# Attention decode with gradients: scores as 512-column matmuls in four column groups, with q among 32 weight columns and rows spread by one-hot fp32 matmuls

One core of one Trainium2 chip. The metric is the device time of one execution in microseconds (us); the kernel before takes a median of 1289.56 us in 3 runs (1288.37 to 1290.94). "Per head" means per one of the 64 pairs of batch and head; a head has eight slots on TensorE, four for its k tile and four for its v tile, and a slot handles a chunk of 16 blocks of 128 rows.

## The reference

One query row per head attends to 8192 keys; wanted are the output and the gradients of q, k and v for a given output gradient.

```python
B, H, Sq, Sk, D = 2, 32, 1, 8192, 128          # all bfloat16
def forward(q, k, v):
    p = softmax(einsum("bhqd,bhkd->bhqk", q, k) * D ** -0.5)
    return einsum("bhqk,bhkd->bhqd", p, v)
out, vjp = jax.vjp(forward, q, k, v)
return out, *vjp(grad_out)                      # out, dq, dk, dv
```

k and v are read (268 MB) and dk and dv written (268 MB). Everything else is small.

## The kernel before

Each head's k and v come as tiles `[128, 64, 128]` of 2 MB; twelve such buffers rotate, and dk or dv is computed in place of k or v and stored from there. TensorE transposes 16 blocks at a time into PSUM, ScalarE copies them to SBUF (`ev`), and the scores are 16 matmuls, each with a transposed block as weights and one column of q as the moving data. The result already has the layout that softmax needs: score of row (p, n) at partition p, column n.

```python
def transpose_chunk(i, c):                       # one slot of TensorE
    ...
    for t in range(CH):                          # CH = 16
        nc.tensor.transpose(tp[:, t, :], src[:, c * CH + t, :], ident_bf[:])
    nc.scalar.copy(out=ev[:], in_=tp[:])

def score_chunk(i, c, ev):
    dst = h.dp if w else h.s                     # w = 0: q.k, w = 1: grad_out.v
    for t in range(CH):
        nc.tensor.matmul(dst[:, c * CH + t : c * CH + t + 1],
                         lhsT=ev[:, t, :], rhs=qdT[:, w, i : i + 1], start=True, stop=True)

def acc(i, w, c):                                # weighted sum of rows, two column groups
    for m in range(CH // QT):                    # QT = 4, so four 512-column matmuls
        nc.tensor.matmul(h.acc[w][g : g + CW, :], lhsT=wts[:, n0 : n0 + CW],
                         rhs=rows[:, n0 : n0 + QT, :] ...)

def outer(i, w, c, ends):                        # VectorE: dk or dv in place, then its store
    ...
    if w == 0 and i in SPREAD:                   # SPREAD = range(4, 60, 7): eight heads
        by_rows(store_eng, dst, h.tile[w], (P - 2, 2))   # store split into 126 + 2 rows
    else:
        eng.dma_start(out=dst[...], in_=h.tile[w][...])

# order of one slot in the main loop:
#   outer products; broadcast of q or grad_out; transposes of this chunk;
#   joins; acc (v, then k); max_spread + expo; scores of the chunk before; small sums
```

Of the kernel before, what the change touches and what calls it, by code (L numbers as in the profile page):

```python
# [11 lines left out]
BF16 = mybir.dt.bfloat16  # L12
F32 = mybir.dt.float32

CH = 16
QT = 4
CW = 64
NG = 2
NTILE = 12
FIRST = 6  # L20
SPREAD = range(4, 60, 7)
# [3 lines left out]
def kernel(  # L25
# [11 lines left out]
    nc = tc.nc  # L37
    B, H, Sq, D = q.shape
    Sk = k.shape[2]
    P = nc.NUM_PARTITIONS  # L40
    assert Sq == 1 and D == P
    BH = B * H
    assert BH <= P
    NT = Sk // P
    assert NT * P == Sk and NT % CH == 0
    NCH = NT // CH
    SL = 2 * NCH
# [4 lines left out]
    pin = tc.keep_in_program_order  # L52

    const = ctx.enter_context(tc.tile_pool(name="const", bufs=1))
    kvp = ctx.enter_context(tc.tile_pool(name="kv", bufs=1))
    evp = ctx.enter_context(tc.tile_pool(name="ev", bufs=2))
    work = ctx.enter_context(tc.tile_pool(name="work", bufs=1))
    small = ctx.enter_context(tc.tile_pool(name="small", bufs=2))
    ps_tp = ctx.enter_context(tc.tile_pool(name="ps_tp", bufs=2, space=bass.MemoryType.PSUM))
    ps_sdp = ctx.enter_context(tc.tile_pool(name="ps_sdp", bufs=1, space=bass.MemoryType.PSUM))  # L60
# [15 lines left out]
    heads = [Head() for _ in range(BH)]  # L76

    def slot_of(i, w):

        n = 2 * i + w  # L80
        return n if n < NTILE else slot_of(i - NTILE // 2, 1 - w)

# [7 lines left out]
    def load(i, w, pieces=(NCH,)):  # L90
        h = heads[i]
        t = kvp.tile([P, NT, D], BF16, tag=f"kv{slot_of(i, w)}", name="kvt")
        h.tile[w] = t
        src = (v_v if w else k_v)[i]
        c = 0
        for m in pieces:
            n0, n1 = c * CH, (c + m) * CH
            pin(load_eng.dma_start(out=t[:, n0:n1, :], in_=src[:, n0:n1, :]))  # L98
            c += m
# [4 lines left out]
    for w, a in enumerate((q, grad_out)):  # L104
        rows = a.rearrange("b h s d -> (b h s) d")
        r0 = FIRST if w == 0 else 0
        if r0:
# [3 lines left out]
                    out=qd_nat[:r0, w, :], in_=rows[:r0], max_dma_last_dim=D  # L111
# [4 lines left out]
    load(0, 1)  # L116
    for j in range(1, min(NTILE // 2, BH)):
        load(j, 0)
# [4 lines left out]
    ident_f = const.tile([P, P], F32)  # L123
    masks.make_identity(nc, ident_f[:])
    ones = const.tile([P, 1], F32)
    nc.vector.memset(ones[:], 1.0)
    groups = [g * P // NG for g in range(NG)]
    diag = const.tile([P, QT], F32)
# [7 lines left out]
    nc.vector.memset(E_pad[:], 0.0)  # L136
    nc.vector.memset(dS_pad[:], 0.0)

    qdT = const.tile([P, 2, BH], BF16)
    for w in range(2):  # L140
        tps = ps_m.tile([P, BH], BF16, tag=f"acc{w}", name="tps")
        nc.tensor.transpose(tps[:], qd_nat[:BH, w, :], ident_bf[:BH, :BH])
        nc.vector.tensor_copy(out=qdT[:, w, :], in_=tps[:])

    dqT = const.tile([P, BH], BF16)
    oT = const.tile([P, BH], BF16)

    def begin_s(i):

        h = heads[i]  # L150
        sw = ps_sdp.tile([P, NT + P + 1], F32, tag="s", name="sw")
        h.s = sw[:, 0:NT]
        h.mT = sw[0:1, NT : NT + P]
        h.mb = sw[:, NT + P :]

    def begin_dp(i):

        h = heads[i]
        dpw = ps_sdp.tile([P, NT + 2 + D], F32, tag="dp", name="dpw")
        h.dp = dpw[:, 0:NT]  # L160
        h.lsum = dpw[:, NT : NT + 2]
        h.qbp = dpw[:, NT + 2 :]

    def broadcast(i, w):

        h = heads[i]
        pin(
            nc.tensor.matmul(  # L168
                h.qbp,
                lhsT=qdT[:, w, i : i + 1].to_broadcast([P, P]),  # L170
                rhs=ident_bf[:],
                start=True,
                stop=True,
            )
        )
        h.qb[w] = small.tile([P, D], BF16, tag=f"qb{w}", name="qb")
        pin(nc.vector.tensor_copy(out=h.qb[w][:], in_=h.qbp))  # L177

    def transpose_chunk(i, c):
        w, c = divmod(c, NCH)  # L180
        src = heads[i].tile[w]
        tp = ps_tp.tile([P, CH, P], BF16, tag="tp", name="tp")
        for t in range(CH):
            pin(nc.tensor.transpose(tp[:, t, :], src[:, c * CH + t, :], ident_bf[:]))  # L184
        ev = evp.tile([P, CH, P], BF16, tag="ev", name="ev")
        pin(nc.scalar.copy(out=ev[:], in_=tp[:]))  # L186
        return ev

    def score_chunk(i, c, ev):
        h = heads[i]  # L190
        w, c = divmod(c, NCH)
        dst = h.dp if w else h.s
        for t in range(CH):
            pin(
                nc.tensor.matmul(  # L195
                    dst[:, c * CH + t : c * CH + t + 1],
                    lhsT=ev[:, t, :],
                    rhs=qdT[:, w, i : i + 1],
                    start=True,
                    stop=True,  # L200
                )
            )

    def max_part(i):
        h = heads[i]
        h.mp = small.tile([P, 1], F32, tag="mp", name="mp")
        pin(nc.vector.reduce_max(out=h.mp[:], in_=h.s, axis=AX.X))  # L207
# [120 lines left out]
    def acc(i, w, c):  # L328
# [6 lines left out]
        for m in range(CH // QT):  # L335
            n0 = c * CH + m * QT
            g = groups[m % NG]
            pin(
# [3 lines left out]
                    rhs=rows[:, n0 : n0 + QT, :].rearrange("p n d -> p (n d)"),  # L342
                    start=(c == 0 and m < NG),
                    stop=(c == NCH - 1 and m >= CH // QT - NG),
                )
# [42 lines left out]
    def outer(i, w, c, ends):  # L388

        h = heads[i]  # L390
        n0 = c * CH
        shape = [P, CH, D // 2, 2]
        pin(
            nc.vector.tensor_tensor(  # L394
                out=h.tile[w][:, n0 : n0 + CH, :].rearrange("p n (e t) -> p n e t", t=2),
                in0=h.qb[w][:]
                .rearrange("p (e t) -> p e t", t=2)
                .unsqueeze(1)
                .to_broadcast(shape),
                in1=h.pair[w][:, n0 : n0 + CH, :].unsqueeze(2).to_broadcast(shape),  # L400
                op=ALU.mult,
            )
        )
        if c + 1 in ends:
            at = ends.index(c + 1)
            b0, b1 = (ends[at - 1] if at else 0) * CH, (c + 1) * CH
            dst = (dv_v if w else dk_v)[i]
            if w == 0 and i in SPREAD:
                by_rows(store_eng, dst, h.tile[w], (P - 2, 2))
            else:  # L410
                eng = load_eng if len(ends) > 1 else store_eng
                pin(eng.dma_start(out=dst[:, b0:b1, :], in_=h.tile[w][:, b0:b1, :]))  # L412
# [6 lines left out]
    last = list(range(1, NCH + 1))  # L419
    AHEAD = NTILE // 2  # L420

    prev = None
    for g in range(SL * BH + O0 + NCH + 4 - SL):
        now = [(g // SL - b, g % SL + b * SL) for b in range(4)]
        now = [(i, r) for i, r in now if 0 <= i < BH]

        def at(r0):

            return next((i for i, r in now if r == r0), None)

        def within(r0):

            return next(((i, r - r0) for i, r in now if r0 <= r < r0 + NCH), None)

        if (i := at(O1 + NCH)) is not None and i + AHEAD < BH:
            load(i + AHEAD, 0)
        if (i := at(O0 + NCH)) is not None and i + AHEAD < BH:
            load(i + AHEAD, 1)
        if x := within(O1):
            outer(x[0], 1, x[1], last if x[0] == BH - 1 else whole)  # L440
        if x := within(O0):
            outer(x[0], 0, x[1], last if x[0] == BH - 1 else whole)
        ev = None
        if g < SL * BH:
            i, r = divmod(g, SL)
            if r == 0:
                begin_s(i)
            if r == 3:
                begin_dp(i)
                broadcast(i, 1)  # L450
            if r == 6:
                broadcast(i, 0)
            ev = transpose_chunk(i, r)
        if (i := at(A1 + NCH + 2)) is not None:
            join(i, 1)
        if (i := at(A0 + NCH + 2)) is not None:
            join(i, 0)
        if x := within(A1):
            acc(x[0], 1, x[1])
        if x := within(A0):  # L460
            acc(x[0], 0, x[1])
        if (i := at(NCH + 2)) is not None:
            max_spread(i)
            expo(i)
        if prev is not None:
            score_chunk(*prev)
        prev = (g // SL, g % SL, ev) if ev is not None else None

        if (i := at(NCH)) is not None:
            max_part(i)  # L470
        if (i := at(NCH + 1)) is not None:
            max_all(i)
        if (i := at(NCH + 3)) is not None:
            normalise_p(i)
        if (i := at(SL)) is not None:
            weigh(i)
        if (i := at(SL + 1)) is not None:
            normalise_ds(i)
        if (i := at(A1 + NCH)) is not None:
            pick(i, 1)  # L480
        if (i := at(A0 + NCH)) is not None:
            pick(i, 0)

    for w, (src, dst) in enumerate(((dqT, out_1), (oT, out_0))):
        tps = ps_m.tile([BH, P], BF16, tag=f"acc{w}", name="tps")
# [34 lines left out]
```

## Time and profile before

| | before |
|---|---|
| median of 3 runs | 1289.56 us |
| profiled run, a fast one | 1284.86 us (span 1283.1) |
| compulsory bytes | 536.9 MB |
| need of TensorE per head, first heads | 17.31 us |
| heads apart later, at the pace of the loads | 19.94 us |

The slices, waits and stretches stand in the prediction below. Four more lines of the page of the kernel before matter later: the busy times, two of the transfer queues (packets, MB, share of the 16 transfer engines' span), and the whole-tile stores (size, median us from issue to landing).

### The profile page before, as it was taken

How to read it: one execution, taken by the hardware profiler on the slowest of the kernel's cores; microseconds unless marked ns; L12 is line 12 of the kernel's file. 1: busy time of each engine (PE TensorE's matmuls, PEld its weight loads, DVE VectorE, ACT ScalarE, POOL GpSimd, SP SyncE). 2: the span in 40 equal slices, each digit the busy share in tenths (PEclk: the TensorE clock that was granted, in tenths of full speed). 3: DMA queues.
4: the chain of work that ended last, by engine and by line, in shares of the span. 5: the costliest groups of instructions: out<-in, count | busy, mean ns of one | idle time of the engine just before them, and what ended most of it. 6: DMA issues, size and time to landing. Idle time of an engine off the chain costs nothing.

```text
span 1283.1 us, 42576 instructions
## 1 busy us (share of the span) xinstructions
PE 1128.5 (88%) x19268; PEld 859.1 (67%) x19268; DVE 935.2 (73%) x2122; ACT 975.2 (76%) x641; POOL 76.0 (6%) x143
## 2 busy tenths in 40 slices
PE   6999999999988998898889898898889888989881
PEld 5777777667666766676666676676667666667650
DVE  2888888778777777686777687786767677777773
ACT  6888888778877877787777787786778677778750
POOL 0000000000000000000000000000000000000000
PEclk9999999999999999998999999998989899899985
DMA  9999999999999999999999999999999999999996
GB/s 388 422 428 426 428 426 427 428 428 425 428 428 425 418 427 428 428 421 427 428 426 425 426 429 428 425 425 429 427 425 421 423 427 428 423 425 426 428 409 267
DMA packets 40194, 539.68 MB, mean 421 GB/s; under 512 B 5196, under 2 KB 5196, under 8 KB 6476
## 3 DMA queue, kind: packets, MB, share of 16 engines
q1 hardware_dynamic: 20172, 272.70, 50.0%
q0 software_dynamic: 19840, 264.25, 48.8%
q8 instruction: 150, 2.46, 0.7%
q14 instruction: 32, 0.26, 0.0%
HBM read 268.47 MB, written 268.47 MB: 418 GB/s over the span
## 4 chain that ended last, share of the span: by engine, by line
DMA 33%; another core or an unknown queue 29%; PE 16%; issue 10%; DVE 8%; ACT 1%; SPq 1%; POOL 1%; POOLq 0%; DVEq 0%; ACTq 0%
DMA kvt<-in_v_dram 20%; DMA out_dram<-kvt 7%; PE tp L184 7%; DVE kvt L394 5%; DMA kvt<-in_k_dram 5%; PE acc L339 4%; PE dpw L195 2%; PE sw L195 2%; DVE sel L362 1%; ACT ev L186 1%; SPq L98 1%; DMA qd_nat<-in_q_dram 1%; PE dpw L282 1%; POOL out_dram L412 0%
## 5 line engine op out<-in xcount | busy, mean ns | idle before, releaser
L186 ACT COPY ev<-tp 128x2048 bf16<-128x2048 bf16 x512 | 954.4, 1865 | 268.8 <-PE tp L184 256.8
L184 PE MATMUL tp<-ident_bf,kvt 128*128 128x128 bf16 x8192 | 558.5, 223 | 96.6 <-DMA kvt<-in_v_dram 74.4
L394 DVE TENSOR_TENSOR kvt<-qb,pair 128x2048 bf16<-128x2048 bf16 x512 | 621.2, 1214 | 0.3
L184 PEld LDWEIGHTS <-kvt 128*128 128x128 bf16 x8192 | 489.8, 101 | 103.6 <-DMA kvt<-in_v_dram 77.8
L195 PEld LDWEIGHTS <-ev 128*128 128x128 bf16 x8192 | 243.2, 96 | 208.7 <-issue 149.1
L339 PE MATMUL acc<-kvt,dS_pad 128*64 128x512 bf16 x1024 | 166.8, 408 | 0.8 <-DVE dqT L379 0.8
L339 PE MATMUL acc<-kvt,E_pad 128*64 128x512 bf16 x1024 | 160.5, 394 | 0.0
L195 PE MATMUL dpw<-qdT,ev 128*128 128x1 bf16 x4096 | 140.7, 164 | 18.8 <-DVE qb L177 18.0
L362 DVE SCALAR_TENSOR_TENSOR sel<-acc,diag,sel 128x128 f32<-128x128 f32 x384 | 134.7, 351 | 13.6
L195 PE MATMUL sw<-qdT,ev 128*128 128x1 bf16 x4096 | 141.8, 164 | 1.2 <-ACT ev L186 1.2
L207 DVE TENSOR_REDUCE mp<-sw 128x1 f32<-128x64 f32 x64 | 14.4, 224 | 156.1 <-PE sw L195 156.1
L412 POOL DMA_DIRECT2D out_dram<-kvt x118 | 63.3, 536 | 1086.1 <-DVE kvt L394 818.4
L339 PEld LDWEIGHTS <-dS_pad 128*64 128x64 bf16 x1024 | 37.4, 110 | 24.4 <-issue 5.3
L247 DVE CAST E_pad<-E_f 128x64 bf16<-128x64 f32 x64 | 12.5, 195 | 54.5 <-ACT E_f L238 54.5
L339 PEld LDWEIGHTS <-E_pad 128*64 128x64 bf16 x1024 | 36.4, 108 | 21.3 <-issue 0.7
L376 PE MATMUL acc<-ones,sel 128*128 128x1 f32 x256 | 43.5, 239 | 6.2 <-DVE sel L362 6.2
L253 DVE CUSTOM_DVE_ANT_0 junk<-E_f,dpw 128x64 bf16<-128x64 f32 x64 | 14.1, 221 | 45.3 <-PE dpw L195 45.3
L282 PE MATMUL dpw<-ld,ones 128*128 128x1 f32 x256 | 46.3, 250 | 0.1
L376 PEld LDWEIGHTS acc<-ones,sel 128*128 128x128 f32 x256 | 39.3, 194 | 7.3 <-DVE sel L362 7.3
L356 DVE TENSOR_SCALAR sel<-acc,diag 128x128 f32<-128x128 f32 x128 | 44.1, 344 | 0.0
L177 DVE CAST qb<-dpw 128x128 bf16<-128x128 f32 x128 | 35.4, 277 | 6.2 <-PE dpw L168 6.2
L282 PEld LDWEIGHTS dpw<-ld,ones 128*128 128x128 f32 x256 | 38.2, 188 | 0.5 <-DVE ld L253 0.5
(44 smaller groups left out, 314.2 us busy)
## 6 DMA issues: line engine op xcount, KB each, us to landing
out_dram<-kvt POOLq DMA_DIRECT2D x118, 2048.0 KB, 68.0
kvt<-in_v_dram SPq DMA_DIRECT2D x64, 2048.0 KB, 19.4
kvt<-in_k_dram SPq DMA_DIRECT2D x63, 2048.0 KB, 19.7
out_dram<-kvt POOLq DMA_DIRECT2D x8, 2016.0 KB, 73.2
out_dram<-kvt SPq DMA_DIRECT2D x8, 512.0 KB, 22.1
kvt<-in_k_dram SPq DMA_DIRECT2D x2, 512.0 KB, 4.5
kvt<-in_k_dram SPq DMA_DIRECT2D x1, 1024.0 KB, 7.3
out_dram<-kvt POOLq DMA_DIRECT2D x8, 32.0 KB, 72.6
```

The source lines that it names most:

```text
L177: pin(nc.vector.tensor_copy(out=h.qb[w][:], in_=h.qbp))
L184: pin(nc.tensor.transpose(tp[:, t, :], src[:, c * CH + t, :], ident_bf[:]))
L186: pin(nc.scalar.copy(out=ev[:], in_=tp[:]))
L195: nc.tensor.matmul(dst[:, c * CH + t : c * CH + t + 1], lhsT=ev[:, t, :], rhs=qdT[:, w, i : i + 1], start=True, stop=True,)
L207: pin(nc.vector.reduce_max(out=h.mp[:], in_=h.s, axis=AX.X))
L282: nc.tensor.matmul(out, lhsT=ones[:].to_broadcast([P, P]), rhs=col, start=True, stop=True)
L339: nc.tensor.matmul(h.acc[w][g : g + CW, :], lhsT=wts[:, n0 : n0 + CW], rhs=rows[:, n0 : n0 + QT, :].rearrange("p n d -> p (n d)"), start=( ...
L356: nc.vector.tensor_scalar(out=h.sel[:], in0=block, scalar1=diag[:, 0:1], scalar2=None, op0=ALU.mult)
L362: nc.vector.scalar_tensor_tensor(out=h.sel[:], in0=block, scalar=diag[:, b : b + 1], in1=h.sel[:], op0=ALU.mult, op1=ALU.add,)
L376: nc.tensor.matmul(h.acc[w][:, 0:1], lhsT=h.sel[:], rhs=ones[:], start=True, stop=True)
L394: nc.vector.tensor_tensor(out=h.tile[w][:, n0 : n0 + CH, :].rearrange("p n (e t) -> p n e t", t=2), in0=h.qb[w][:] .rearrange("p (e t) -> ...
L412: pin(eng.dma_start(out=dst[:, b0:b1, :], in_=h.tile[w][:, b0:b1, :]))
```

## The change

The intent is to replace sixteen weight loads and one-column matmuls per slot by four 512-column matmuls. q becomes one of 32 weight columns; q's columns of the heads stand four apart with zeros between, so the window of 32 columns also holds the next heads' q. It starts c columns early for chunk c, so that the wanted scores of chunk c accumulate in row c of their group; the rows from 4 on belong to other heads and are never used. Four column groups of 32 write four row ranges of one PSUM bank and may run together. After four chunks the bank holds a head's scores as rows; VectorE copies it to SBUF, and four fp32 matmuls with one-hot columns pick rows 0 to 3 of each group and transpose them into the layout of before.

```diff
-    qdT = const.tile([P, 2, BH], BF16)
+    qdT = const.tile([P, 2, Q0 + NCH * BH + SW], BF16)      # q's columns NCH apart, zeros between
...
     def score_chunk(i, c, ev):
-        dst = h.dp if w else h.s
-        for t in range(CH):
+        q0 = Q0 + NCH * i - c
+        for g in range(SG):                                  # SG = 4, SW = 32
             pin(nc.tensor.matmul(
-                    dst[:, c * CH + t : c * CH + t + 1],
-                    lhsT=ev[:, t, :],
-                    rhs=qdT[:, w, i : i + 1],
-                    start=True, stop=True,
+                    h.raw[g * SW : (g + 1) * SW, :],
+                    lhsT=qdT[:, w, q0 : q0 + SW],
+                    rhs=ev[:, g * QT : (g + 1) * QT, :].rearrange("p n d -> p (n d)"),
+                    start=(c == 0), stop=(c == NCH - 1),
             ))
+    def keep_raw(i):
+        h.rows = work.tile([P, QT * P], F32, tag="rows", name="rows")
+        pin(nc.vector.tensor_copy(out=h.rows[:], in_=h.raw[:]))
+
+    def spread_rows(i, w):
+        for t in range(QT):
+            pin(nc.tensor.matmul(
+                    h.score[w].rearrange("p (n t) -> p n t", t=QT)[:, :, t],
+                    lhsT=h.rows[:, t * P : (t + 1) * P],
+                    rhs=sel4[:].rearrange("p c g -> p (c g)"), start=True, stop=True))
```

Both score areas, the transposed maximum, the sums and the broadcast of q and grad_out (`broadcast`) now share one PSUM bank, since `raw` needs one for itself. The maximum, the exponentials and everything after them come one slot later (cut here; in the main loop, `NCH + 2` becomes `NCH + 3` and so on). TensorE has 19268 matmuls before and 14148 after. (The trace lists each fp32 matmul twice.)

More of the change, by code (lines that the diff above doesn't have):

```diff
@@ L18 @@
 NG = 2
+SG = 4
+SW = 32
 NTILE = 12
@@ L137 @@
     nc.vector.memset(dS_pad[:], 0.0)
-    qdT = const.tile([P, 2, BH], BF16)
+    sel4 = const.tile([P, NCH, SG], F32)
+    nc.vector.memset(sel4[:], 0.0)
+    for g in range(SG):
+        nc.vector.tensor_copy(
+            out=sel4[g * SW : (g + 1) * SW, :, g],
+            in_=ident_f[g * SW : (g + 1) * SW, g * SW : g * SW + NCH],
+        )
+    Q0 = NCH - 1
+    qdT = const.tile([P, 2, Q0 + NCH * BH + SW], BF16)
+    nc.vector.memset(qdT[:], 0.0)
     for w in range(2):
@@ L142, with begin @@
         nc.tensor.transpose(tps[:], qd_nat[:BH, w, :], ident_bf[:BH, :BH])
-        nc.vector.tensor_copy(out=qdT[:, w, :], in_=tps[:])
+        nc.vector.tensor_copy(
+            out=qdT[:, w, Q0 : Q0 + NCH * BH].rearrange("p (i f) -> p i f", f=NCH)[:, :, 0],
+            in_=tps[:],
+        )
     dqT = const.tile([P, BH], BF16)
     oT = const.tile([P, BH], BF16)
-    def begin_s(i):
+    def begin(i):
         h = heads[i]
-        sw = ps_sdp.tile([P, NT + P + 1], F32, tag="s", name="sw")
-        h.s = sw[:, 0:NT]
-        h.mT = sw[0:1, NT : NT + P]
-        h.mb = sw[:, NT + P :]
-    def begin_dp(i):
-        h = heads[i]
-        dpw = ps_sdp.tile([P, NT + 2 + D], F32, tag="dp", name="dpw")
-        h.dp = dpw[:, 0:NT]
-        h.lsum = dpw[:, NT : NT + 2]
-        h.qbp = dpw[:, NT + 2 :]
+        sw = ps_sdp.tile([P, 2 * NT + 2 * P + 4], F32, tag="s", name="sw")
+        h.score = (sw[:, 0:NT], sw[:, NT : 2 * NT])
+        h.s, h.dp = h.score
+        h.mT = sw[0:1, 2 * NT : 2 * NT + P]
+        h.qbp = sw[:, 2 * NT + P : 2 * NT + 2 * P]
+        h.lsum = sw[:, 2 * NT + 2 * P : 2 * NT + 2 * P + 2]
+        h.mb = sw[:, 2 * NT + 2 * P + 2 : 2 * NT + 2 * P + 3]
     def broadcast(i, w):
@@ L169, in broadcast @@
                 h.qbp,
-                lhsT=qdT[:, w, i : i + 1].to_broadcast([P, P]),
+                lhsT=qdT[:, w, Q0 + NCH * i : Q0 + NCH * i + 1].to_broadcast([P, P]),
                 rhs=ident_bf[:],
@@ L191, in score_chunk @@
         w, c = divmod(c, NCH)
-        dst = h.dp if w else h.s
-        for t in range(CH):
+        if c == 0:
+            h.raw = ps_sdp.tile([P, QT * P], F32, tag="raw", name="raw")
+        q0 = Q0 + NCH * i - c
+        for g in range(SG):
             pin(
                 nc.tensor.matmul(
-                    dst[:, c * CH + t : c * CH + t + 1],
-                    lhsT=ev[:, t, :],
-                    rhs=qdT[:, w, i : i + 1],
+                    h.raw[g * SW : (g + 1) * SW, :],
+                    lhsT=qdT[:, w, q0 : q0 + SW],
+                    rhs=ev[:, g * QT : (g + 1) * QT, :].rearrange("p n d -> p (n d)"),
+                    start=(c == 0),
+                    stop=(c == NCH - 1),
+                )
+            )
+    def keep_raw(i):
+        h = heads[i]
+        h.rows = work.tile([P, QT * P], F32, tag="rows", name="rows")
+        pin(nc.vector.tensor_copy(out=h.rows[:], in_=h.raw[:]))
+    def spread_rows(i, w):
+        h = heads[i]
+        for t in range(QT):
+            pin(
+                nc.tensor.matmul(
+                    h.score[w].rearrange("p (n t) -> p n t", t=QT)[:, :, t],
+                    lhsT=h.rows[:, t * P : (t + 1) * P],
+                    rhs=sel4[:].rearrange("p c g -> p (c g)"),
                     start=True,
@@ L445 @@
             i, r = divmod(g, SL)
-            if r == 0:
-                begin_s(i)
-            if r == 3:
-                begin_dp(i)
+            if r == NCH:
+                begin(i)
                 broadcast(i, 1)
-            if r == 6:
+            if r == NCH + 2:
                 broadcast(i, 0)
@@ L461 @@
             acc(x[0], 0, x[1])
-        if (i := at(NCH + 2)) is not None:
+        if (i := at(NCH + 1)) is not None:
+            spread_rows(i, 0)
+        if (i := at(SL + 1)) is not None:
+            spread_rows(i, 1)
+        if (i := at(NCH + 3)) is not None:
             max_spread(i)
@@ L469 @@
         if (i := at(NCH)) is not None:
+            keep_raw(i)
+        if (i := at(SL)) is not None:
+            keep_raw(i)
+        if (i := at(NCH + 1)) is not None:
             max_part(i)
-        if (i := at(NCH + 1)) is not None:
+        if (i := at(NCH + 2)) is not None:
             max_all(i)
-        if (i := at(NCH + 3)) is not None:
+        if (i := at(NCH + 4)) is not None:
             normalise_p(i)
-        if (i := at(SL)) is not None:
+        if (i := at(SL + 1)) is not None:
             weigh(i)
-        if (i := at(SL + 1)) is not None:
+        if (i := at(SL + 2)) is not None:
             normalise_ds(i)
```

## The prediction

> **What bounds the kernel now.** I read the page's shares first: TensorE 88%, ScalarE 76%, VectorE 73% of 1283.1 us. That reads like a TensorE kernel. The slices below it say otherwise.
>
> ```profile
> PE   6999999999988998898889898898889888989881
> DMA  9999999999999999999999999999999999999996
> GB/s 388 422 428 426 428 426 427 428 428 425 428 428 425 418 427 428 428 421 427 428 426 425 426 429 428 425 425 429 427 425 421 423 427 428 423 425 426 428 409 267
> HBM read 268.47 MB, written 268.47 MB: 418 GB/s over the span
> ```
>
> The transfers stand at about 427 GB/s from the second slice to the last but two, whether TensorE shows a 9 or an 8. The bytes are the inputs and outputs themselves, 536.9 MB; at 427 GB/s they take 1257 us, and 26 us are left for the start and the end. So I looked at what TensorE does in its gaps: the table of waits.
>
> ```profile
> POOL out_dram L412 <- DVE kvt L394: 818.4, 89, 31.5
> ACT ev L186 <- PE tp L184: 256.8, 370, 9.3
> PE tp L184 <- DMA kvt<-in_v_dram: 74.4, 40, 5.5
> PE tp L184 <- DMA kvt<-in_k_dram: 22.2, 31, 1.5
> SPq L98 <- DMA out_dram<-kvt: 1139.0, 116, 25.1
> ```
>
> TensorE waits for loads (96.6 us), ScalarE for TensorE, and the load queue for stores that must land before a buffer is free (1139 us; the twelve 2 MB buffers are all in use). Stores take a median of 68.0 us from issue to landing, loads 19.4: seven or so tiles stand in the transfer queues. That is the slack: computation can be later by tens of us before a transfer is late.
>
> The table of stretches shows two regimes. First number: length, then busy time of PE, PEld, DVE, ACT, POOL, and at the end granted clock, DMA share, GB/s.
>
> ```profile
> 100.00:120.00 20.00, 19.68 (x360) 15.04 (x357) 17.25 (x39) 17.60 (x12) 1.88 (x3) 1.00 1.01 429
> 640.00:660.00 20.00, 17.11 (x303) 13.14 (x301) 14.37 (x34) 15.04 (x11) 1.93 (x3) 1.00 1.01 427
> 1260.00:1283.00 23.00, 0.90 (x3) 0.63 (x3) 0.92 (x5) 0.00 (x0) 0.00 (x0) 0.50 0.51 211
> ```
>
> Early, twelve tiles were loaded ahead and TensorE works them off at its own pace: starts of transposes from head to head lie 17.31 us apart for heads 1 to 12. From about 215 us on it gets ahead of the loads, and heads come 19.94 us apart (mean of heads 20 to 63). So the compute side has 17.31 us of need in a period of 19.94 us: **2.6 us per head of slack**. The end is fixed by the last tile, landed at 1233.5, its work until 1260, and stores that drain at half rate until 1283.
>
> **What the Trainium skill says.** "DMA: Bandwidth & Descriptors", section Bandwidth, gives a ceiling of 435 GB/s and 425 measured for one core; the trace's 427 agrees, so nothing is to be had there without fewer bytes. "TensorE: Matmul & The Clock Gate", Part 3, says that matmuls whose outputs lie in different column groups run at the same time (2.38 times for three groups at 512 columns). The trace agrees for two groups: below, four 512-column matmuls on two halves take 0.62 us, and the score work after them starts 0.55 us after their start; its Part 2 gives 216 ns for one, 0.86 us for four in a row. "TensorEngine Tiling (Array Packing)", Key Properties, says that changing the tiling mode drains the array: the trace has 0.31 us from the second pair's start to the first score matmul, where pair to pair is 0.24. Four groups are not in this trace; I rest on the page. "VectorE: DVE Perf Modes", the errata section, gives 120 + columns cycles at 0.96 GHz for a copy out of PSUM: 258 ns for 128 fp32 columns; the trace has 277.
>
> **The change, part by part.** One slot of TensorE (one chunk of 16 tiles; eight slots to a head) in the compute-bound stretch:
>
> ```profile
> 117.96 1.05 PE L184 MATMUL tp<-ident_bf,kvt 128*128 128x128 bf16 x16
> 118.94 0.62 PE L339 MATMUL acc<-kvt,E_pad 128*64 128x512 bf16 x4
> 119.50 0.55 PE L195 MATMUL sw<-qdT,ev 128*128 128x1 bf16 x16
> 119.92 1.05 PE L184 MATMUL tp<-ident_bf,kvt 128*128 128x128 bf16 x16
> ...
> 125.69 0.38 PE L218 MATMUL sw<-gm,ones 1*128 1x1 f32 x2
> 126.39 0.54 PE L195 MATMUL dpw<-qdT,ev 128*128 128x1 bf16 x16 [0.32 <-DVE qb L177]
> ```
>
> From start to start: transposes 0.98, accumulation 0.56, scores 0.41 us; 1.95 us, times 8 is 15.6, and the small fp32 matmuls and one wait make the 17.3.
>
> 1. Scores. Removed: 16 weight loads with one-column matmuls, 0.41 us. Added: four weight loads of 32 columns and four 512-column matmuls in four column groups, one wave. If the groups run together, the wave costs what the second pair does, 0.31 us to the next kind of work, perhaps 0.35. Estimate -0.08 x 8 = **-0.6 us per head**. The instruction order shows 2048 of them where 8192 were.
> 2. Spreading the rows. Eight fp32 matmuls per head (128x128 weights, 16 columns). The kernel has the like in its fp32 sums over partitions: at 111.43 two passes take until 111.65, 0.22 us per matmul, bound by the fp32 weight load, so that 16 columns for one should be nearly free. 8 x 0.22, plus two switches of mode at 0.1: **+2.0 us per head**.
> 3. Waits. The wait for the broadcast copy (about 0.4 us at 126.39) goes, as scores have a bank of their own: -0.4. But exponentials move one slot later while their accumulation does not. Before, the padded weights are ready about 3.55 us after the slot's transposes start; after the change TensorE would want them at 0.98 + 0.56 + 0.29 + 0.35 + 0.98 = 3.16: **+0.4**. All small outputs now share one bank, and the transposed maximum follows closely on a broadcast copy that VectorE reaches late: +0.2.
> 4. VectorE: two copies of 128x512 fp32 per head, each 277 + 384/0.96 = 677 ns by the trace's 277 ns: +1.36 us on 14.6 us per head, 16.0. Below TensorE. ScalarE is unchanged (15.4).
>
> Sum: 17.3 - 0.6 + 2.0 - 0.4 + 0.4 + 0.2 = **18.9 us per head** of compute need, against 19.94 of transfers. All of it lies beside transfers: the slack falls from 2.6 to about 1 us. TensorE's backlog of loaded tiles is then worked off far more slowly, perhaps never; this changes no byte rate. Break-even: the last head's transposes start at 1223.4 us now, (1223.4 - 9.4)/63 = 19.3 us per head.
>
> At the end the last head's dS comes one slot and a 0.68 us copy later: +1 to 2 us of computation, mostly under the store backlog. If TensorE lags, the last loads arrive earlier and more of the tail overlaps: a few us less. I let these cancel.
>
> **Rivals.** (a) Column groups run one after the other: the wave costs 0.86 + 0.1 instead of 0.35, +0.6 x 8 = +4.9, 23.8 us per head, time about 1290 + 64 x (23.8 - 19.3) = 1578. Against it: the pairs of this very trace overlap. 4%. (b) fp32 spreads or the new waits cost more than read here, the need passes 19.3 and TensorE becomes the bound: 19.8 gives +32 us, 1322. For it: the margin is only 0.4 us to break-even and I count three waits that no trace shows. 8%, of which a part is under 2%. (c) TensorE was the bound after all, as its 88% suggests, and 6144 fewer matmuls bring some per cent: against it stand 427 GB/s and the waits for loads; and by my sum TensorE has more to do, not less. 2%. (d) The tail's half-rate drain falls differently, 5 us either way.
>
> **Range and chances.** Centre: before, 1289.56, less nothing: 1289. Low end 1279: a better overlapped tail. High end 1306: short transfer queues with some bubbles, or break-even passed by a quarter of a us (16 us). Faster by over 2% would need bytes or rate to change: 0.02. Slower by over 2% (from 1315) is (a) and the worse part of (b): 0.09. Same: 0.89.
>
> **What would show it.** Right: GB/s still about 427 in the middle slices; waits of TensorE for loads smaller than 96.6 us and the early regime longer than 215 us, its heads 18.2 to 19.3 us apart; spreads near 0.9 us per group of four; the score wave about 0.35 us to the next transposes; a new wait of the accumulation for E_pad; VectorE's busy time up by some 87 us. Wrong: slices below 420 GB/s in the middle, or the queue for stores idle because VectorE's products come late.

## More of the kernel before

```profile
PE 1128.5 (88%) x19268; PEld 859.1 (67%) x19268; DVE 935.2 (73%) x2122; ACT 975.2 (76%) x641; POOL 76.0 (6%) x143
...
q8 instruction: 150, 2.46, 0.7%
q14 instruction: 32, 0.26, 0.0%
...
out_dram<-kvt POOLq DMA_DIRECT2D x118, 2048.0 KB, 68.0
```

The q8 line is easily passed over: the core's own instructions are fetched by the same sixteen transfer engines, 150 times 16 KB for TensorE. It is 0.7% of the engines' time.

## The result, and the profile after

All outputs are correct. The changed kernel took a median of 1280.01 us in 4 runs (1279.29 to 1282.0), the kernel before 1288.96 in its 4 (1285.78 to 1290.94). The ratio is 0.9935 (95%: 0.9912 to 0.9959). The verdict is "same" (within 2%), and the time lies in the predicted range, near its low end. But the gain of 0.65% is outside the interval of chance, and the centre had said none.

The page of the changed kernel:

```profile
PE 1190.2 (93%) x14148; PEld 810.6 (63%) x14148; DVE 1025.8 (80%) x2256; ACT 975.3 (76%) x641; POOL 76.0 (6%) x143
...
GB/s 392 423 428 428 428 427 429 430 426 429 427 430 425 414 427 429 428 423 428 428 429 419 425 428 426 427 421 427 427 423 421 427 429 428 420 425 428 428 411 273
...
q8 instruction: 110, 1.80, 0.5%
q14 instruction: 33, 0.27, 0.1%
...
L208 PE MATMUL raw<-ev,qdT 128*32 128x512 bf16 x2048 | 205.2, 391 | 1.5 <-ACT ev L196 1.5
L221 DVE COPY rows<-raw 128x512 f32<-128x512 f32 x128 | 88.6, 692 | 22.4 <-PE raw L208 22.4
...
out_dram<-kvt POOLq DMA_DIRECT2D x118, 2048.0 KB, 40.6
```

TensorE and VectorE are busier than before, not less. The rate of the slices is that of before. Stores land 27 us sooner after issue, because products come later and queue less. And TensorE's instructions are fetched in 40 transfers fewer.

Its table of stretches, for the first two stretches that the prediction used (length, busy time of PE, PEld, DVE, ACT, POOL, then granted clock, DMA share, GB/s):

```profile
100.00:120.00 20.00, 19.04 (x230) 12.73 (x229) 16.22 (x37) 15.79 (x11) 1.06 (x2) 1.00 1.01 430
640.00:660.00 20.00, 19.04 (x234) 13.14 (x232) 16.54 (x37) 15.78 (x11) 1.31 (x3) 1.00 1.01 427
```

The two regimes of before have become one: 19.04 of 20 us in both. Heads come 19.45 us apart from beginning to end. TensorE is always the later one, and still the transfer engines are full at 427 GB/s, as work in the queues covers it. The waits of the changed kernel (us in total, times, longest) agree: no wait of TensorE for a load is left, and there are new ones.

```profile
DVE E_pad L280 <- ACT E_f L271: 80.3, 64, 2.1
...
PE sw L178 <- DVE mp L240: 38.2, 63, 0.8
...
PE acc L372 <- DVE E_pad L280: 24.5, 64, 1.4
```

The timeline of TensorE in the changed kernel (start, duration, instruction, and in brackets the idle time before it):

```profile
102.79 0.40 PE L208 MATMUL raw<-ev,qdT 128*32 128x512 bf16 x4
103.12 1.07 PE L194 MATMUL tp<-ident_bf,kvt 128*128 128x128 bf16 x16
104.55 0.62 PE L372 MATMUL acc<-kvt,E_pad 128*64 128x512 bf16 x4 [0.36 <-DVE E_pad L280]
...
107.21 1.06 PE L228 MATMUL sw<-sel,rows 128*128 128x16 f32 x8
108.20 0.40 PE L208 MATMUL raw<-ev,qdT 128*32 128x512 bf16 x4
...
118.19 0.22 PE L178 MATMUL sw<-ident_bf,qdT 128*128 128x128 bf16 x1 [0.60 <-DVE mp L240]
```

Four score matmuls of 512 columns start 3 to 4 ns apart and the next work starts 0.33 us after them: the four column groups do run together. Four spreading matmuls take 0.99 us from their start to the next work.

**Where did 6 to 9 us go?** In whole GB/s, the slices of the middle don't show it. So both kernels were cut into the same three stretches at the end. Before:

```profile
1262.00:1270.00 8.00, 0.00 (x0) 0.00 (x0) 0.04 (x1) 0.00 (x0) 0.00 (x0) 0.50 0.61 254
1270.00:1274.00 4.00, 0.00 (x0) 0.00 (x0) 0.00 (x0) 0.00 (x0) 0.00 (x0) 0.50 0.49 209
1274.00:1280.00 6.00, 0.00 (x0) 0.00 (x0) 0.00 (x0) 0.00 (x0) 0.00 (x0) 0.50 0.44 180
```

After:

```profile
1262.00:1270.00 8.00, 2.57 (x14) 1.42 (x14) 6.82 (x12) 0.00 (x0) 0.00 (x0) 0.63 0.99 401
1270.00:1274.00 4.00, 0.01 (x1) 0.00 (x0) 0.35 (x2) 0.00 (x0) 0.00 (x0) 0.50 0.51 200
1274.00:1280.00 6.00, 0.00 (x0) 0.00 (x0) 0.00 (x0) 0.00 (x0) 0.00 (x0) 0.50 0.05 20
```

In the kernel before, computation is over at 1262 and half of the transfer engines have nothing left, while the other half works on until about 1280. Share 0.5 is not every engine at half speed: in the transfer records, an engine's 16 KB transfers follow one another back to back every 607 ns, so each engine's last one can be followed, and eight engines end near 1262.5 and eight near 1280.4. In the changed kernel the early eight get their last work from the later computation, to about 1270, and the late eight end at 1273.9, as a median: one of them goes on alone to 1278.2 (the 0.05 of the last stretch), and this profile is of the slowest of the four runs. So what has to be explained is why the *late* eight end 6.5 us sooner.

The end is only where it shows. By the transfer records the last load's data are in at 1229.2 us instead of 1232.4 (in e11 below at 1223.3, in e2 at 1238.9; but in e9, the changed kernel with a straggler, at 1235.7), so part of the difference has built up before, at tenths of a per cent of the rate. And the late engines are late all along: from 400 to 1200 us the sixteen parts of a store in the kernel before land 43 us apart (median), seven of them together as the last. That is a good part of the 68.0 us that a store takes.

### The profile page after: what moved, and what is told of

The parts are those of the page before. It is cut to its first block, busy times and chain, and to the rows that moved or that the text cites. A ratio compares the mean times of both kernels' runs of the same rounds, so it can differ in the third digit from the quotient of the medians. Undisturbed runs are those within 1.5% of the kernel's fastest.

```text
span 1280.2 us, 32473 instructions
## 1 busy us (share of the span) xinstructions
PE 1190.2 (93%) x14148; PEld 810.6 (63%) x14148; DVE 1025.8 (80%) x2256; ACT 975.3 (76%) x641; POOL 76.0 (6%) x143
## 4 chain that ended last, share of the span: by engine, by line
PE 59%; DVE 16%; ACT 10%; issue 10%; DMA 4%; POOL 0%; SPq 0%; ACTq 0%; POOLq 0%; DVEq 0%
PE tp L194 24%; PE acc L372 15%; ACT ev L196 9%; PE raw L208 9%; DVE kvt L427 6%; PE sw L228 4%; DVE sel L395 4%; DMA out_dram<-kvt 3%; DVE rows L221 3%; PE sw L315 3%; PE sw L178 2%; PE acc L409 2%; ACT E_f L271 1%; DVE sel L389 1%; DVE E_pad L280 1%
## 5 line engine op out<-in xcount | busy, mean ns | idle before, releaser
L194 PE MATMUL tp<-ident_bf,kvt 128*128 128x128 bf16 x8192 | 544.4, 220 | 0.0
L208 PE MATMUL raw<-ev,qdT 128*32 128x512 bf16 x2048 | 205.2, 391 | 1.5 <-ACT ev L196 1.5
L372 PE MATMUL acc<-kvt,E_pad 128*64 128x512 bf16 x1024 | 160.2, 393 | 24.5 <-DVE E_pad L280 24.5
L228 PEld LDWEIGHTS sw<-sel,rows 128*128 128x128 f32 x1024 | 124.7, 192 | 52.4 <-DVE sel L395 25.9
L395 DVE SCALAR_TENSOR_TENSOR sel<-acc,diag,sel 128x128 f32<-128x128 f32 x384 | 134.8, 351 | 13.6
L208 PEld LDWEIGHTS <-qdT 128*32 128x32 bf16 x2048 | 53.1, 93 | 136.6 <-issue 131.8
L228 PE MATMUL sw<-sel,rows 128*128 128x16 f32 x1024 | 137.1, 266 | 0.0
L221 DVE COPY rows<-raw 128x512 f32<-128x512 f32 x128 | 88.6, 692 | 22.4 <-PE raw L208 22.4
L178 PE MATMUL sw<-ident_bf,qdT 128*128 128x128 bf16 x128 | 28.5, 223 | 38.2 <-DVE mp L240 38.2
L246 DVE TENSOR_REDUCE gm<-sw 1x1 f32<-1x128 f32 x64 | 17.9, 279 | 55.4 <-PE sw L244 55.4
L315 PEld LDWEIGHTS sw<-ld,ones 128*128 128x128 f32 x256 | 38.1, 188 | 29.7 <-issue 15.0
L315 PE MATMUL sw<-ld,ones 128*128 128x1 f32 x256 | 49.1, 261 | 0.0
## 6 DMA issues: line engine op xcount, KB each, us to landing
out_dram<-kvt POOLq DMA_DIRECT2D x118, 2048.0 KB, 40.6
```

Of the source, the lines that this page charges most:

```text
L194: pin(nc.tensor.transpose(tp[:, t, :], src[:, c * CH + t, :], ident_bf[:]))
L208: nc.tensor.matmul(h.raw[g * SW : (g + 1) * SW, :], lhsT=qdT[:, w, q0 : q0 + SW], rhs=ev[:, g * QT : (g + 1) * QT, :].rearrange("p n d -> ...
L221: pin(nc.vector.tensor_copy(out=h.rows[:], in_=h.raw[:]))
L228: nc.tensor.matmul(h.score[w].rearrange("p (n t) -> p n t", t=QT)[:, :, t], lhsT=h.rows[:, t * P : (t + 1) * P], rhs=sel4[:].rearrange("p ...
L315: nc.tensor.matmul(out, lhsT=ones[:].to_broadcast([P, P]), rhs=col, start=True, stop=True)
L395: nc.vector.scalar_tensor_tensor(out=h.sel[:], in0=block, scalar=diag[:, b : b + 1], in1=h.sel[:], op0=ALU.mult, op1=ALU.add,)
```

## The experiments

Two theories to start with. **Pace**: the changed kernel's slower and even pace keeps the transfer queues shorter, and that makes for a better end. **TensorE work**: fewer matmuls help after all. Later a third, **fetches**: what counts is the number of instruction transfers of q8, because they take the time of transfer engines that are the bound. Below, "late eight" is the median end of the eight late engines in the profiled run, from the transfer records.

**e1, control.** The kernel before, unchanged.

> The kernel before, unchanged, as a control: how far its own runs and profiles scatter. Before's seven-odd runs so far went from 1284.9 to 1290.9 us and its one profile is of the fastest of them, while the changed kernel's four went from 1279.3 to 1282.0. Every theory: ratio 1.000 within 0.3%. Of use is the second profile: if the lost transfer time (span less bytes over 427 GB/s, 19.1 us in the first profile) is again spread as 3 us at the start, some 3 in the middle and 13 at the end, then the end decides.

1286.33 us against 1285.66, ratio 1.0002 (0.9988 to 1.0016). Late eight at 1280.2. So ratios of a few tenths of a per cent can be told apart with five rounds.

**e2, the kernel before at a slower pace.** Four or five of a chunk's transposes are done twice (38 per head; the expectation says 39).

```diff
-        for t in range(CH):
+        again = 5 if c else 4
+        for t in list(range(again)) + list(range(CH)):
```

> The kernel before, with 39 transposes per head done twice (result unchanged), so that TensorE's own pace falls from 17.31 to about 17.31 + 39 x 0.0557 = 19.48 us per head, the pace that the changed kernel shows (19.45). It has 4992 more TensorE matmuls and weight loads than before. Pace theory (the gain of 9 us comes from TensorE pacing the stores at just under the transfers' rate, so that the store queue stays short: 40.6 us to landing instead of 68.0): 1278 to 1283 us, store landing about 40 us, heads 19.5 apart throughout. Rival, fewer instructions to fetch (0.65 MB less, 1.5 us) or fewer matmuls: 1289 to 1292 us.

1289.96 us, ratio 1.0036 (1.0021 to 1.0052): slower, where the pace theory wanted it faster. The pace missed its aim (19.06 us per head in the first 40 heads, 19.48 expected), and the stores landed sooner than before, though not as soon as in the changed kernel (55.5 us; 68.0 and 40.6). Late eight at 1283.6. That speaks against the pace theory; e3 decides it. What also changed is that the page lists more fetches:

```profile
span 1289.6 us, 47440 instructions
...
q8 instruction: 169, 2.77, 0.8%
```

**e3, the changed kernel at a faster pace.** `rows` and `sel4` in bf16, so that a spread takes one pass; and the second broadcast moved behind the accumulation, away from the maximum.

```diff
-    sel4 = const.tile([P, NCH, SG], F32)
+    sel4 = const.tile([P, NCH, SG], BF16)
-        h.rows = work.tile([P, QT * P], F32, tag="rows", name="rows")
+        h.rows = work.tile([P, QT * P], BF16, tag="rows", name="rows")
-            if r == NCH + 2:
-                broadcast(i, 0)                  # was before transpose_chunk
+        if (i := at(NCH + 2)) is not None:
+            broadcast(i, 0)                      # now after acc
```

> The changed kernel with the rows and the one-hot in bf16 (scores rounded to bf16; results may differ slightly) and the second broadcast behind the transposes, so that the wait for the maximum goes: pace about 19.45 - 1.2 - 0.67 = 17.5 us per head, that is, the same slack as before with the new score matmuls. Pace theory: back to 1285 to 1290 us, stores landing after 60 to 70 us, TensorE waiting for loads again from about 220 us on. Rival (fewer instructions, or the score matmuls themselves): stays at 1279 to 1282 us.

Correct, 1279.94 us, ratio to before 0.9956 (0.994 to 0.9972). The pace went from 19.45 to 18.01 us per head (17.5 expected: the wait for the maximum moved to the next user of the bank), stores again take 66.7 us to land, and the computation ends 13.6 us earlier than in the changed kernel, at 1256.7 instead of 1270.3. The time is that of the changed kernel. So pace is neither the gain's cause nor, up to 19.45 us, a cost.

**e4, the changed kernel at a slower pace.** Two transposes per chunk done twice.

```diff
-        for t in range(CH):
+        again = 2
+        for t in list(range(again)) + list(range(CH)):
```

> The changed kernel with two transposes of every chunk done twice: pace 19.45 + 16 x 0.0557 = 20.34 us per head. If TensorE is now what the end hangs on: the last head's start moves by 62 x 0.89 = 55 us, 1335 us (+4%), with transfers under 420 GB/s in the middle slices. If transfers still bound it (period 19.65 us at 427 GB/s): 1280 + 62 x (20.34 - 19.65) = 1323 at least. If TensorE had slack left, 1280.

1318.13 us, ratio 1.0249 (1.0235 to 1.0263), pace 20.11: less loss than either theory of a loss expected, partly as the pace stayed under the 20.34 meant. Here TensorE has become the bound: the transfer rate falls below 300 GB/s in the last slices. If 63 heads of 20.11 us end at 1318.1, one at 19.45 would make 1318.1 - 63 x 0.66 = 1276.5, which is just what the transfers allow. So the break-even is at about 19.5 us per head and the changed kernel stands on it.

**e5, half of the score instructions in the kernel before.** Two columns per matmul instead of one, 8 instead of 16 per chunk. Wrong results (relative error 1.02); the transfers and all dependencies are those of before.

```diff
-        for t in range(CH):
+        i0 = min(i, BH - 2)
+        for t in range(0, CH, 2):
...
-                    dst[:, c * CH + t : c * CH + t + 1],
+                    dst[:, c * CH + t : c * CH + t + 2],
-                    rhs=qdT[:, w, i : i + 1],
+                    rhs=qdT[:, w, i0 : i0 + 2],
```

> The kernel before with 8 score matmuls of two columns per chunk instead of 16 of one (every second column is wrong on purpose). Nothing of the change's structure is in it; 4096 matmuls and as many weight loads less. The pace theory has fallen: the paced kernel before took 1290.0, the fast changed kernel 1279.9. New theory, instruction fetch: TensorE's instructions arrive in 16 KB transfers (150 before, 110 in the changed kernel, 169 paced, 106 fast), and the eight transfer engines that finish last end at 1280.5, 1273.7, 1284, 1273 us in that order, 0.175 us per such transfer. It expects about 118 of them and 1285.7 - 32 x 0.175 = 1280.1 us, ratio 0.9956. Rival, the gain is in the change's layout (score matmuls into a bank of their own, dS one slot later, the tail): 1285.7, ratio 1.000.

1281.13 us against 1286.75, ratio 0.9955 (0.9939 to 0.997), as the fetch theory expected; that the fourth digit agrees is luck, given the interval. Its TensorE only waits longer for loads than before (126.5 us for v's instead of 74.4). 4096 matmuls and 4096 weight loads are gone, and with them 32 fetches: 64 bytes per instruction.

```profile
q8 instruction: 118, 1.93, 0.6%
```

**e6, e3 with more TensorE instructions.** 48 one-column matmuls more per head, overwritten afterwards.

```diff
+        for _ in range(24 if c == 0 else 0):
+            pin(nc.tensor.matmul(h.raw[0:SW, 0:1], lhsT=qdT[:, w, q0 : q0 + SW],
+                                 rhs=ev[:, 0, 0:1], start=True, stop=True))
```

> The fast changed kernel with 48 one-column matmuls per head more, whose output is overwritten (result unchanged): 6144 more TensorE instructions, 24 more fetch transfers, about 130; pace 18.0 + 1.2 = 19.2 us per head, no slower than the changed kernel's 19.45 that cost nothing. Fetch theory: 1279.9 + 24 x 0.175 = 1284.1 us, ratio 0.999. Rival (layout): stays at 1280, ratio 0.9956.

Correct, 1283.95 us, ratio to before 0.9975 (0.9959 to 0.9991): 4 us of e3's gain are given back, by work that fits in TensorE's slack. 130 fetches instead of 106, late eight at 1277.0 instead of 1272.9.

**e7, the changed kernel without split stores.**

```diff
-SPREAD = range(4, 60, 7)
+SPREAD = range(0)
```

> The changed kernel without the eight stores that are split into 126 and 2 rows. If the end hangs on the single most loaded transfer engine, and the split was there to relieve one: 16 rows of 16 KB at 0.61 us go back to it, up to 9.7 us: 1280 to 1290 us. If the sum of bytes over all engines sets the end: no change, ratio 0.9935 to 0.9956 as for the changed kernel.

1294.87 us, ratio 1.0057 (1.0043 to 1.0071): worse than the expected range. Fifteen engines end at about 1282 and one alone at 1291.4. The stretches show it (0.20 of sixteen engines over 13 us, of which one engine all along is 0.06 and the rest are the first two microseconds):

```profile
1270.00:1280.00 10.00, 5.34 (x23) 1.72 (x19) 9.76 (x18) 0.00 (x0) 0.00 (x0) 0.50 0.99 399
1280.00:1293.00 13.00, 0.90 (x3) 0.63 (x3) 1.27 (x5) 0.00 (x0) 0.00 (x0) 0.50 0.20 79
```

So which engine is late depends on how stores are cut, and the splits of the kernel before are worth 15 us in the changed one too. The halves of eight are no law of the chip.

**e8, twelve split stores instead of eight.**

```diff
-SPREAD = range(4, 60, 7)
+SPREAD = range(4, 64, 5)
```

> The changed kernel with twelve split stores instead of eight. Single-engine theory: eight engines finish together at 1273.7, so relieving one more cannot help: ratio unchanged within 0.2%, or 1 to 3 us slower if an engine that takes the two rows is one of the late ones. An improvement of over 3 us would say that one engine alone is last.

1289.6 us, ratio 1.002 (0.9998 to 1.0042): a miss; some 10 us slower than the changed kernel, where at most 3 were expected. The late engines end from 1275.5 to 1282.7, more unequal than in the changed kernel's first profile but for its one straggler (1273.2 to 1274.2, and 1278.2).

**e9, the changed kernel again**, beside e10.

> The changed kernel unchanged, a control beside the fast one and for the slope: 110 fetch transfers. Fetch theory: 1286 - 40 x 0.175 = 1279 us, ratio 0.9945, within 0.2% of the fast kernel's 0.9956.

1280.09 us (1278.12 to 1289.75), ratio 0.9956 (0.9929 to 0.9983). The gain is confirmed on another chip, at 6.2 us. The slow run was the profiled one: at the same pace, one engine alone ended at 1285.9. Single runs can have such a straggler, and no profile here tells why.

**e10, more instructions on GpSimd.** Nine small memsets per slot on the least busy engine, into a spare column of `qdT`; 4725 instructions more.

```diff
+        for _ in range(9):
+            pin(nc.gpsimd.memset(qdT[:, 1, QW : QW + 2], 0.0))
```

> The changed kernel with 72 tiny GpSimd memsets per head into a spare column (about 4700 instructions, 0.3 MB; TensorE's stream is the same but for 128 rows). It asks whether fetched bytes matter whoever executes them. If all fetched instructions load the transfer engines alike: 18 fetch transfers of 16 KB more (or 36 of 8 KB) and +3.2 us against the changed kernel run beside it. If only TensorE's own instruction count matters (its pace, its semaphores): no change, within 0.1%. If the memsets hold stores back: store landings and gaps change, and the run says nothing on fetches.

1280.07 us, ratio 0.9952 (0.9934 to 0.9971): equal to e9 on the same chip. The page:

```profile
q8 instruction: 110, 1.80, 0.5%
q14 instruction: 70, 0.57, 0.1%
```

37 more fetches on q14, 8 KB each, show no cost, where "all fetches cost alike" expected 3.2 us; the late eight end at about 1273.7, as in the changed kernel. The intervals (2.4 us either way here, 3.5 in e9) are about as wide as the 3.2 us, though, and in the transfer records those q14 fetches that can be followed alternate between two engines, so they could hardly move the end of eight. That a fetch for GpSimd is free where it runs isn't shown.

**e11, a quarter of the score instructions in the kernel before.** As e5 with four columns, 4 matmuls per chunk. Wrong results (relative error 1.24).

```diff
-        for t in range(CH):
+        i0 = min(i, BH - 4)
+        for t in range(0, CH, 4):                # dst t : t + 4, rhs i0 : i0 + 4
```

> The kernel before with 4 score matmuls of four columns per chunk (three of four columns are wrong on purpose): 6144 matmuls and as many weight loads less than before, about 102 fetch transfers on TensorE's queue. Nothing of the change's layout is in it, and TensorE's pace is near 15 us per head, the most slack of all. If the end follows the number of these transfers in a line (0.175 us each, as 118, 130, 150 and 169 did): 1286.3 - 48 x 0.175 = 1277.9 us, ratio 0.9935, the late eight engines done at about 1272. If something else takes over at about 1280 (106 and 110 transfers gave 1279.9 and 1280.1): 1280 to 1281, ratio 0.9955.

1277.0 us, ratio 0.9919 (0.9899 to 0.994). The gain goes on, the plateau at 0.9955 falls, and the line's 0.9935 is inside the interval. (The pace missed: the first heads come 17.2 us apart, as before, not 15.)

```profile
q8 instruction: 102, 1.67, 0.5%
```

**e12, e3 with eight k loads cut by rows** into 112, 8 and 8, in the hope of giving the early eight engines more and the late eight less.

```diff
+        if w == 0 and i in range(8, 64, 7):
+            by_rows(load_eng, t, src, (P - 16, 8, 8))
+            return
```

> The fast changed kernel with eight of its k loads split into 112, 8 and 8 rows. [...]8 x 0.61 = 4.9 us of work moved off eight engines onto the eight others. Theory that the end hangs on eight engines that finish 10 to 15 us late: if these are the upper eight, 1279.9 - 4.9 = 1275 us, a ratio near 0.992; if they are the lower eight, +4.9, 1285 us. If the end does not hang on the balance of the engines: no change, 0.9956.

1290.29 us, ratio 1.0028 (1.001 to 1.0045), 10 us slower than e3. It settles nothing on the halves: the loads themselves suffered (34.7 us from issue to landing instead of 19.6). Each piece of 8 rows did run on eight engines (the trace has 128 more completion records than e3's, eight for each of the 16 pieces), but which eight it doesn't name.

**The runs together**, in order of TensorE's fetches (time against the kernel before of the same rounds, by medians):

| run | fetches (q8) | late eight end, us | time - before, us |
|---|---|---|---|
| e11, before, quarter of the scores (wrong) | 102 | 1271.8 | -8.9 |
| e3, changed, faster pace | 106 | 1272.9 | -5.7 |
| changed | 110 | 1273.9 | -6.2 (e9), -9.0 (first) |
| e10, changed, more on GpSimd | 110 | 1273.7 | -6.2 |
| e5, before, half of the scores (wrong) | 118 | 1274.7 | -5.6 |
| e6, changed, faster pace, more matmuls | 130 | 1277.0 | -2.8 |
| before | 150 | 1280.4 (e1: 1280.2) | 0 |
| e2, before, repeated transposes | 169 | 1283.6 | +4.3 |

The third column is close to a line: (1283.6 - 1271.8) / (169 - 102) = 0.176 us per fetch, though it mixes two kernels, paces from 17.3 to 19.45 us per head, and more or less work on TensorE. The last column follows it with a scatter of 2 to 3 us, as the stragglers would make one expect. Not in the table are e4, where TensorE is the bound, and e7, e8 and e12, whose stores or loads are cut otherwise: with 106 or 110 fetches they took 3 to 8 us longer than the kernel before, so the line holds only for the same cuts.

## Why the prediction was right, and where not

**Right: the bound and the small effect.** Transfers were the bound before and after: 427 GB/s in the middle slices of both, whatever TensorE's share. That share rose from 88 to 93% while the time fell.

**Right: most of the parts.** The score wave was to take 0.31 to 0.35 us to the next work; it takes 0.33. So rival (a), column groups in series, is out. Four spreads were to take "near 0.9 us"; 0.99. VectorE was to gain some 87 us; it gained 90.6 (1025.8 - 935.2), with the copy at 692 ns instead of 677. The wait of the accumulation for `E_pad` came, with 0.4 us per head (24.5 us in 64 waits is 0.38, and the slot with it is 0.44 us longer), and TensorE's waits for loads went.

**Mis-sized: the shared bank.** The term "the transposed maximum follows closely on a broadcast copy that VectorE reaches late: +0.2" was three times too small, and the wait stands the other way round: the second broadcast waits for the row maximum, as both touch the shared bank, and the slot with it loses 0.67 us (38.2 us in 63 waits is 0.61 of that). With it the sum is 17.31 - 0.67 (score waves) + 1.99 (spreads) + 0.44 + 0.67 - 0.41 (the old wait for the broadcast copy) = 19.33 us; measured are 19.45, not 18.9. e3, in which only the spreads' passes and this wait's place were changed, came down to 18.01, and not to 17.5, as part of the wait moved on to the next user of the bank.

**Right by luck: the margin.** The prediction put break-even at 19.3 us per head. The changed kernel needs 19.45, so by its own figures it should have been some 64 x 0.15 = 10 us slower. It was not, because break-even is at about 19.5: the figure of 19.3 took the last head's place in the kernel before, 1223.4 us, as the latest allowed, whereas eight engines were still draining 18 us longer than computation needed. e4 shows the edge: 20.11 us cost 38 us. Rival (b) was one wait away.

**Wrong: "Centre: before, 1289.56, less nothing".** The step that failed is the one that counts only the inputs and outputs as load on the transfer engines ("nothing is to be had there without fewer bytes"). The engines also fetch the program. A TensorE fetch of 16 KB takes a transfer engine about 0.98 us (median; 0.95 in the changed kernel), a data transfer of the same size 0.611 us (median). The change removes 5120 matmuls and as many weight loads, 10240 x 64 B = 40 x 16 KB, as the pages show: 150 and 110. At 0.176 us each on the late eight, that is 7.0 us; measured are 6.2 and 9.0. The low end of the range, 1279, stood there for "a better overlapped tail"; that the time came near it is luck. Removing score instructions from the kernel before (e5, e11) brought a like gain, adding TensorE instructions (e2, e6) took time or took it back, and pace (e3) did nothing. In this sense rival (c), "fewer matmuls bring some per cent", was right in the sign of 0.65% and wrong in its reason: TensorE was not the bound and has more to do now.

**Wrong: "I let these cancel".** The later computation at the end costs nothing, because it lies under the late eight's drain; but it uses up that cover. The last small outputs are issued at 1270.3 and take 8.1 us to land, against 1261.9 and 18.1 before: the changed kernel's end is now set about as much by its computation as by the late engines. e3 leaves 14 us there at the same time.

**Which engines carry the fetches.** The transfer records name no engine, but since transfers follow one another at fixed distances, a fetch can often be followed back to its engine's last store, and the landing of that store's sixteen parts ranks the engine. In the kernel before, between 200 and 1220 us, 55 of 65 such fetches sit on the seven engines where the store lands last (of data transfers followed in the same way, 39%), and 7 on the one where it lands first. In the changed kernel 32 of 40 sit on the last eight (data: 45%), 7 on the first; e1 to e3, e5, e6 and e8 to e12 agree (79 to 89% on the last eight). In e4 and e7 the parts of a store land too close together or in another order, and the count doesn't carry over. So some eight engines carry TensorE's fetches, and they are the late ones, all but one: an estimate of 150 x 0.98 / 8 = 18.4 us of fetches on each, near the 17.9 us by which the late eight end later.

**What stays open.** Why the fetches run on these engines, no run shows; e7 and e8 show that the ends hang on how stores are cut too, and e12 failed to shift them. Nor is the size of one fetch's effect explained in full: 40 fetches are 40 x 0.98 = 39 us of engine time, 4.9 us over eight engines, and the late eight ended 6.5 us sooner. In e5 and e11 the stores' own transfers also took some 46 us less in total (9.98 ms, not 10.03), which no theory here says. That is as much as their missing fetches took (33 and 49 us), so these two runs don't test fetches alone; in the changed kernel and in e2 the stores' time is that of before. And fetches can't be told from the number of TensorE instructions, since each one is fetched; that the cost lies in the fetch and not in some other by-product of an instruction is argued from where it shows (on the engines that carry the fetches, with TensorE idle by the end), not shown by itself. No correct version beat the changed kernel clearly; e3 equals it with 1.4 us per head more to spare.

## What to carry to other kernels

In a kernel that is bound by transfers, look at the instruction queues in the page as well as the data: thousands of tiny TensorE instructions are transfers too, and fewer, larger ones can pay a little even when TensorE gets busier. Before moving outputs into one PSUM bank, ask for every pair of them which engine will wait for which; here that cost three times its estimate and almost all of the margin. When the DMA share falls to a fraction at the end, see whether all engines are slower or some have finished: only what the late ones carry counts.

## What the Trainium skill lacked or had wrong

- "Runtime: NRT & Kernel Launch", Instruction fetch mechanics, has the blocks of 16 KiB (256 instructions) and calls the cost of going from one to the next mostly hidden. It leaves out the data transfers, and "DMA: Bandwidth & Descriptors" has no cost for a fetch either. Here TensorE's fetches took a transfer engine about 0.98 us each (data of that size: 0.611 us), sat mostly on the late engines (55 of 65), and each went with about 0.176 us at the end of the run.
- "DMA: Bandwidth & Descriptors" says that the engines of a transfer finish independently and that two of them are usually slower; no page has halves. Here about eight ended near 1262.5 and eight near 1280.4 us in the kernel before, and without split stores one alone ended at 1291.4, some 9 us after the others.
- "TensorE: Matmul & The Clock Gate", Part 3, gives a figure for column groups alone only for three. Four work as well: 512-column matmuls started 3 to 4 ns apart, with 0.33 us to the next work, where four of its 216 ns would be 0.86.
- "TensorEngine Tiling (Array Packing)", Key Properties, says that a change of mode drains the array, without a size: 0.31 us to the next kind of work instead of 0.24 to the next pair, so at most about 0.07 us here.
- "FP8 and Floating Point Precision", in its notes on TensorE, gives true fp32 four passes, without a time; the traces list each fp32 matmul twice (8 records for the four spreads), and four of 128x128 with 16 columns took 0.99 us.
